# Batch 0's first DFT in whole float32, its result kept in chip memory and read from there

## The chip, the cores and the metric

The kernel runs on one NeuronCore of one Trainium2 chip. The metric is device time of one execution in microseconds: 2584.85 us, the median of three runs (2584.58 to 2585.59). Lower is better.

Names used below: PE (TensorE, the matmuls) and PEld (its weight loads), DVE (VectorE), ACT (ScalarE), POOL (GpSimd), SP (SyncE, which issues the DMAs). Chip memory means the on-chip memory of 128 partitions; DRAM is the memory outside the core.

## What is computed

A spectral layer on 8 batches of 3008 x 256, and behind it a feed-forward layer (FFN) on all 24064 rows:

```
X = rfft(x, axis=1)
Yr = Xr @ w_r - Xi @ w_i + b_r
Yi = Xr @ w_i + Xi @ w_r + b_i
Y  = shrink(Yr, 0.01) + 1j * shrink(Yi, 0.01)
y  = irfft(Y, n=3008, axis=1)
h  = y @ w_in          # 256 -> 2048
g  = h - tanh(h)
out = g @ w_out        # 2048 -> 256
```

The result is float32 and w_in and w_out are float64. Where the kernel needs the precision of float32 it either lets PE multiply whole float32 operands, or splits an operand into a high and a low part (type fp32r) and adds three matmuls: high x low, high x high, low x high.

## The kernel before

**The spectral layer by stages.** 3008 = 64 x 47, so the DFT of a batch is done in two steps. F1 (class `Forward`) is the DFT of length 47: x is laid out as [94 rows (two interleaved series of 47), 32 pairs, 256], and the table f1 [94, 96] turns 94 rows into 96. One step `q` treats two pairs, one matmul of N = 512. The result `a` has 32 pairs x 96 rows x 256. F2 (class `Spectrum`, for batch 0 its subclass `WholeSpectrum`) is the DFT of length 64: it needs the same row j of all 32 pairs on the partitions of chip memory, so F1's result is written to DRAM as `a` and read back in another order as `at`. The 96 rows of `a` are 4 groups of 24; a unit `jp` (12 units a batch) takes rows 2 jp and 2 jp + 1 of each group: 4 x 32 = 128 partitions and 2 x 256 columns. `rows` (L316) is this view of `a`. Behind F2 a unit does the products with w_r and w_i (`cross`), `shrink`, and the first step of the inverse DFT (`inverse`), and writes `z` to DRAM (`put`). Class `Unit` reads z back and makes the time rows that the FFN takes.

**Batch 0 at the start** (L930 to L972 and L973 to L1057). No FFN work exists yet, so batch 0 runs alone. PE first gets 11 matmuls on zeros (`idle(11)`), which keep it busy until x arrives. The 8 pieces of x are loaded at once. Each of the 16 steps (`steps`) splits its two pairs (ACT makes the high part, DVE the low), does three matmuls and one `idle(1)`, and `keep` copies the result from the accumulators into a buffer `st` and sends it to `a` in DRAM: 16 buffers taken in turn from three tags (th with 2, k with 5, tmp with 4). Between these writes the loads of the bias, w_i, w_r and i1 are issued. Then come `idle(16)` and the loop over 12 units: in iteration i unit i does F2 (`dft`), unit i - 1 `cross`, unit i - 2 `shrink`, unit i - 3 `inverse`; the load of `at` for unit i + 2 is issued in iteration i, into one of three buffers (tag `at`; the first held w_i). Weight pieces are loaded in iterations 0 (two), 4, 5, 8 and 9 (`raw_at`), halves of the table i2 in 5 and 8, and x of batch 1 in 9 and 10. `some` interleaves the conversion of weight pieces from float64.

**Order.** PE, ACT, DVE, POOL and SP run exactly the order in which the program issues their instructions (`manual_schedule`); semaphores come from the data. All DMAs of the program are issued by SP, in order: one that waits holds back all behind it.

**The weights.** `win_h`, `win_l` [128, 2, 2048] and `wout_h`, `wout_l` [128, 16, 256] hold w_in and w_out in two parts, 64 KB of each partition in all. They are filled in 16 pieces (`load_f64`, `split_f64`); pieces of part 0 and 1 are those of the FFN's first 8 of 16 blocks of 128. Pieces 0 to 5 are loaded in the unit loop, the others later, in `early`. `Chunk.up`, `Chunk.down`, `Pair.left` and `weight_sums` read them. The main part of the time is the loop over `Pair`s (L1163 on), where the FFN of one chunk and the spectral units of later batches alternate on PE.

**Buffers of DRAM.** `a` has two buffers that batches take in turn, `z` likewise.

Of the kernel before, what the change touches and what calls it, by code (L numbers as in the profile page):

```python
# [10 lines left out]
F32 = mybir.dt.float32  # L11
# [23 lines left out]
def dft_constants():  # L35
    _, m0 = index_maps()
    j = np.arange(NJ)
    n2 = np.arange(47)
    a = 2 * np.pi * np.outer(n2, j) / 47
    one = np.concatenate([np.cos(a), -np.sin(a)], 1)  # L40
    f1 = np.zeros((94, 96))
    f1[:47, :48] = one
    f1[47:, 48:] = one
    f1s = np.zeros((128, 96))
    f1s[:47, :48] = f1s[:47, 48:] = f1s[64:111, :48] = one
    n1 = np.array([2 * pair + par for par in range(2) for pair in range(NP)])
    th = 2 * np.pi * np.outer(n1, np.arange(128) % 64) / 64
    c, s = np.cos(th).reshape(2, NP, 128), np.sin(th).reshape(2, NP, 128)
    dr = np.stack([c, s], 2).transpose(1, 0, 2, 3).reshape(128, 128)
    di = np.stack([-s, c], 2).transpose(1, 0, 2, 3).reshape(128, 128)  # L50
    f2 = np.concatenate([dr[:, :96], dr[:, 32:], di[:, :96], -di[:, 32:]], 1)
    ph = 2 * np.pi * np.outer(np.arange(64), n1) / 64
    sg = np.where(np.arange(64) < 32, 1.0, -1.0)[:, None]
    c, s = np.cos(ph), np.sin(ph)
    i1 = np.zeros((2, 64, 2, 2, NP))
    i1[0, :, :, 0], i1[0, :, :, 1] = c.reshape(64, 2, NP), s.reshape(64, 2, NP)
    i1[1, :, :, 0], i1[1, :, :, 1] = (-sg * s).reshape(64, 2, NP), (sg * c).reshape(64, 2, NP)
    i1 = i1.transpose(0, 1, 4, 2, 3).reshape(128, 128)
# [12 lines left out]
    i2 = i2.transpose(1, 0, 2).reshape(128, -1)  # L71
    return [np.ascontiguousarray(v, np.float32) for v in (f1, f1s, f2, i1, i2)]


@with_exitstack
def spectral_ffn(ctx, tc, x, w_r, w_i, b_r, b_i, w_in, w_out, x_twice, f1, f1s, f2, i1, i2, out):
    nc = tc.nc
# [62 lines left out]

    win_h = const.tile([P, 2, FF], F32R, name="win_h")
    win_l = const.tile([P, 2, FF], F32R, name="win_l")
    wout_h = const.tile([P, NF, D], F32R, name="wout_h")
    wout_l = const.tile([P, NF, D], F32R, name="wout_l")

# [26 lines left out]
    def split_f64(part, k, raw):  # L172
        if k < 2:
            sl = slice(part * WB, (part + 1) * WB)
            hi_out, lo_out = win_h[:, k, sl], win_l[:, k, sl]
        else:
            n = WB // D
            f = part * WB // P + (k - 2) * n
            hi_out, lo_out = (w[:, f:f + n].rearrange("p t e -> p (t e)") for w in (wout_h, wout_l))
        top, low = raw[:, :, 1], raw[:, :, 0]  # L180
# [28 lines left out]
    class Forward:  # L209
# [4 lines left out]
        def load(self):  # L214
            if self.ch == 0:
# [15 lines left out]
        def dft(self, q):  # L231
            xh, xl = self.x[q]
            self.ps[q] = bank("ps_f1")
            pv = self.ps[q][:96].rearrange("p (a d) -> p a d", d=D)
            nc.tensor.matmul(pv, f1l, xh, start=True, stop=False)
            nc.tensor.matmul(pv, f1h, xh, start=False, stop=False)
            nc.tensor.matmul(pv, f1h, xl, start=False, stop=True)

        def keep(self, q, copy=nc.scalar.copy):
            if self.b == 0 or self.b == 1 and self.ch >= LOOK:  # L240
                n = 2
                pool, tag, bufs = ((ffn, "th", 2), (work, "k", 5), (work, "tmp", 4))[(2 * self.ch + q) % 3] if self.b == 0 else (load, "at", 3)
                st = pool.tile([96, 2, D], F32, name="st", tag=tag, bufs=bufs)
            else:
# [67 lines left out]
    class Spectrum:  # L312
# [6 lines left out]
        def load(self):  # L319
            if self.jp == 0:  # L320
                z_dram[self.b] = dram.tile([NP, 96, D], F32, name=f"z_{self.b}", tag="z")
            self.at = load.tile([P, 2, D], F32, name="at", tag="at", bufs=3)
            nc.sync.dma_start(out=self.at.rearrange("p j d -> p (j d)"), in_=rows(a_dram[self.b][0], self.jp))
            if self.b > 2:
# [7 lines left out]
        def transform(self):  # L332
            ps = self.ps = bank("ps_f2")
            pv = ps.rearrange("p (t r j m) -> p t j r m", t=2, r=2, j=2)
            for jj in range(2):
                o = m0[2 * self.jp + jj]
                rhs = f2t.rearrange("p (r u c) -> p r u c", r=2, u=2)[:, :, :, o:o + 32]
                for t in range(2):
# [183 lines left out]
    class Chunk:  # L522
# [27 lines left out]
        def up(self, f, i):  # L550
            n = self.n
            hp = H[0][:, i % 2, :n] if H else early_h[i % 2 if i < SINGLE else 0][:, :n]
            k = 0
            for lhs, rhs in ((win_l, self.yh), (win_h, self.yh), (win_h, self.yl)):
                for t in range(2):
                    nc.tensor.matmul(hp, lhs[:, t, f * P:(f + 1) * P], rhs[:, t, :n], start=k == 0, stop=k == 5)  # L556
                    k += 1
# [10 lines left out]
        def down(self, f, gh, gl, t):  # L568
# [8 lines left out]
            if f == 0 and self.c > 1:  # L577
                self.o[t] = ps_oo.tile([P, 512], F32, name=f"o{t}", tag=f"o{t}")
            for k, (lhs, rhs) in enumerate(((wout_l, gh), (wout_h, gh), (wout_h, gl))):
                nc.tensor.matmul(  # L580
                    self.o[t][:, :n], lhs[:, f, t * P:(t + 1) * P], rhs,
                    start=f == 0 and k == 0, stop=f == NF - 1 and k == 2,
                )
# [41 lines left out]
    class Pair:  # L625
# [13 lines left out]
        def left(self, name):  # L639
# [4 lines left out]
            t, f = {"a11": (0, 0), "a12": (1, 0), "a21": (0, 1), "a22": (1, 1)}[name]  # L644
            return [w[:, t, (2 * q + f) * P:(2 * q + f + 1) * P] for w in (win_h, win_l)]

# [51 lines left out]
    def weight_sums(p):  # L698
        wv = [w.rearrange("p k (q i m) -> p k i q m", i=2, m=P)[:, :, :, 2 * p:2 * p + 2] for w in (win_h, win_l)]
        pair = [work.tile([P, 2, 2, P], F32, name=f"ws{k}", tag="tmp", bufs=4) for k in range(2)]  # L700
# [233 lines left out]
    with tc.manual_schedule(engines={E.PE, E.Activation, E.DVE, E.Pool, E.SP}):  # L934
# [9 lines left out]

        idle(11)
        below = const.tile([P, 1], F32, name="below")
        nc.vector.memset(below, -LAM)
        f1h, f1l = split(load_whole(f1, [94, 96], "f1", tag="tmp", bufs=4), "f1", rest=nc.vector)
        first = [Forward(0, ch) for ch in range(NP // XC)]
        for f in first:  # L950
            f.load()
        f2t = load_const(f2, [P, 384], "f2")
        steps = [(f, q) for f in first for q in range(XC // 2)]
        loads = linear_loads()
        lin_in = next(loads)
        bias = lin_in[2]
        for i in range(len(steps) + 2):
            if 10 <= i < 14:
                next(loads)
# [279 lines left out]
```

## Time and profile before

| | |
|---|---|
| time before, median of three | 2584.85 us |
| profiled execution, its own time | 2586.71 us |
| its span (first to last instruction) | 2584.9 us |
| mean granted clock of PE over the span | 0.997 |
| busy: PE / DVE / ACT / POOL | 2557.7 / 1838.1 / 1608.0 / 792.4 us |
| moved by DMA | 235.87 MB, mean 91 GB/s |

The profile is of one execution. The chain is the work that ended last, followed back from the last instruction. A row of the chain in order of time has start, duration, engine, tile and line; a row of the timeline has start, duration, engine, line, operation, tiles, shapes and count, and in brackets how long the engine was idle before and what released it. A line of stretches has the stretch, its length, each engine's busy time with its count, the granted clock, the mean busy share of the 16 DMA engines, and GB/s. A row of a group has count, busy time, mean ns of one, and idle time before. A row of DMA issues has tiles, queue, count, KB each and the median time from issue to landing. A whole float32 matmul shows as two records.

### The profile page before, as it was taken

The page shows a single profiled execution, that of the slowest core. Times are in us where ns is not written, and L with a number is a line of the kernel's source. Part 1 is how long each engine was busy: PE and PEld are TensorE (multiplying, and loading weights), DVE is VectorE, ACT ScalarE, POOL GpSimd, SP SyncE. Part 2 cuts the span into 40 slices and gives each one's busy share as a digit, 9 for nine tenths or more (in the row PEclk, how much of TensorE's full clock was granted, in tenths as well). Part 3 has the DMA queues.
Part 4 walks back from the last instruction along what each step waited for, and adds up shares of the span by engine and source line. Part 5 has one row for each costly group of instructions (what it writes and reads, how often), then busy time and mean ns, then how long its engine had stood idle before and what let it go on. Part 6 is the DMA issues. An engine that isn't in the chain of part 4 may idle for free.

```text
span 2584.9 us, 42892 instructions
## 1 busy us (share of the span) xinstructions
PE 2557.7 (99%) x16041; PEld 2283.9 (88%) x16041; DVE 1838.1 (71%) x2742; ACT 1608.0 (62%) x2942; POOL 792.4 (31%) x885
## 2 busy tenths in 40 slices
PE   8999999999999999999999999999999999999999
PEld 6787898899889999899999999899998999999998
DVE  6787884777777776777776777767777666666665
ACT  5556566666666666666666666666666555565655
POOL 0004334332334433333324333333333323221210
PEclk8999999999999999999999999999999999999999
DMA  6521225233333332333323342232433121111000
GB/s 192 169 84 56 89 72 152 82 99 97 95 105 118 104 116 82 98 112 107 120 72 115 97 132 90 86 116 84 131 91 95 62 73 60 47 43 47 19 27 17
DMA packets 145521, 235.87 MB, mean 91 GB/s; under 512 B 12192, under 2 KB 85152, under 8 KB 145312
## 3 DMA queue, kind: packets, MB, share of 16 engines
q1 hardware_dynamic: 145312, 233.11, 28.8%
q8 instruction: 127, 2.08, 0.3%
q14 instruction: 82, 0.67, 0.1%
HBM read 142.36 MB, written 90.70 MB: 90 GB/s over the span
## 4 chain that ended last, share of the span: by engine, by line
PE 95%; DVE 2%; DMA 1%; ACT 1%; issue 0%; POOL 0%; SPq 0%; DVEq 0%; ACTq 0%; POOLq 0%
PE o L580 39%; PE H L651 34%; PE ps_v L366 5%; PE ps_i L507 4%; PE ps_f L339 3%; PE ps_t L366 2%; PE he L556 2%; PE ps_f L285 1%; PE ps_v L448 1%; PE ps_i L413 1%; PE ps_i L415 1%; PE ps_i L414 1%; DMA a<-st 1%; PE oe L580 1%; PE ps_t L448 0%; PE ps_i L471 0%
## 5 line engine op out<-in xcount | busy, mean ns | idle before, releaser
L689 ACT CAST gh<-th 128x1024 fp32r<-128x1024 f32 x352 | 371.4, 1055 | 381.8 <-DVE th L685 253.5
L651 PEld LDWEIGHTS H<-y_t,sum 128*128 128x128 f32 x3168 | 516.2, 188 | 102.3 <-DVE th L685 5.5
L580 PE MATMUL o<-gh,wout_l 128*128 128x512 f32 x1408 | 563.2, 400 | 0.0
L580 PE MATMUL o<-gl,wout_h 128*128 128x512 f32 x1408 | 554.3, 394 | 0.5 <-DVE gl L693 0.5
L580 PE MATMUL o<-gh,wout_h 128*128 128x512 f32 x1408 | 552.7, 393 | 0.0
L651 PE MATMUL H<-y_t,sum 128*128 128x256 f32 x3168 | 545.2, 281 | 0.9 <-DVE ot L593 0.7
L693 DVE TENSOR_TENSOR gl<-th,gh 128x1024 fp32r<-128x1024 f32 x352 | 440.6, 1252 | 57.6 <-ACT gh L689 54.8
L685 DVE TENSOR_TENSOR th<-H,th 128x1024 f32<-128x1024 f32 x352 | 428.3, 1217 | 5.0 <-ACT th L682 2.3
L682 ACT ACTIVATE th<-H 128x1024 f32<-128x1024 f32 x352 | 362.6, 1030 | 42.5 <-PE H L651 42.0
L667 DVE TENSOR_TENSOR H<-H,late 128x256 f32<-128x256 f32 x352 | 152.2, 432 | 319.5 <-PE H L651 283.3
L580 PEld LDWEIGHTS o<-gl,wout_h 128*128 128x128 f32 x1408 | 264.7, 188 | 60.8 <-DVE gl L693 1.5
L673 DVE TENSOR_TENSOR H<-H,late 128x256 f32<-128x256 f32 x352 | 151.7, 431 | 191.4 <-PE H L651 183.1
L651 PE MATMUL H<-y_b,win_h 128*128 128x256 f32 x1408 | 280.8, 281 | 0.0
L580 PEld LDWEIGHTS o<-gh,wout_l 128*128 128x128 f32 x1408 | 265.0, 188 | 7.9 <-ACT gh L689 0.5
L580 PEld LDWEIGHTS o<-gh,wout_h 128*128 128x128 f32 x1408 | 264.9, 188 | 7.3
L659 ACT COPY late<-H 128x256 f32<-128x256 f32 x352 | 131.6, 374 | 211.9 <-PE H L651 209.1
L651 PE MATMUL H<-y_more,win_h 128*128 128x256 f32 x1408 | 263.1, 279 | 0.0
L97 POOL TENSOR_TENSOR z_l<-mn,z_h 128x512 fp32r<-128x512 f32 x84 | 112.5, 1340 | 431.3 <-ACT z_h L96 276.4
L651 PEld LDWEIGHTS H<-y_more,win_h 128*128 128x128 f32 x1408 | 215.3, 188 | 6.1
L651 PEld LDWEIGHTS H<-y_b,win_h 128*128 128x128 f32 x1408 | 214.4, 188 | 0.2 <-POOL y_b L97 0.2
L651 PE MATMUL H<-y_more,win_l 128*128 128x256 f32 x704 | 201.1, 286 | 1.2 <-DVE H L673 1.2
L403 DVE TENSOR_TENSOR y<-tb,ps_v 64x256 f32<-64x256 f32 x384 | 160.8, 419 | 56.8 <-PE ps_v L366 44.8
(190 smaller groups left out, 4381.3 us busy)
## 6 DMA issues: line engine op xcount, KB each, us to landing
a<-st SPq DMA_DIRECT2D x188, 192.0 KB, 3.0
x<-in_x_twice SPq DMA_DIRECT2D x55, 512.0 KB, 4.7
at<-a SPq DMA_DIRECT2D x96, 256.0 KB, 3.2
z<-zo SPq DMA_DIRECT2D x96, 256.0 KB, 2.0
zin<-z SPq DMA_DIRECT2D x64, 384.0 KB, 4.4
out<-ot SPq DMA_DIRECT2D x47, 512.0 KB, 3.1
shared<-a SPq DMA_DIRECT2D x60, 256.0 KB, 3.7
shared<-in_i SPq DMA_DIRECT2D x58, 235.0 KB, 4.0
```

The lines of the kernel that those rows point to most:

```text
L97: rest.tensor_tensor(out=lo, in0=src, in1=hi.bitcast(F32), op=ALU.subtract)
L366: nc.tensor.matmul(dst, lhs[:, t], rhs[:, t, :], start=n == 0, stop=n == 5)
L403: nc.vector.tensor_tensor(out=y[ri * 64:(ri + 1) * 64, jj, :], in0=common(jj, ri), in1=self.vv[jj * 64:(jj + 1) * 64, ri * D:(ri + 1) * D] ...
L580: nc.tensor.matmul(self.o[t][:, :n], lhs[:, f, t * P:(t + 1) * P], rhs, start=f == 0 and k == 0, stop=f == NF - 1 and k == 2,)
L651: nc.tensor.matmul(dst, a, b, start=start and k == 0, stop=k == 2, skip_group_check=True)
L659: nc.scalar.copy(out=self.p7, in_=self.c11)
L667: nc.vector.tensor_tensor(out=self.c21, in0=self.acc, in1=self.p7, op=ALU.add)
L673: nc.vector.tensor_tensor(out=self.c22, in0=self.acc, in1=self.p7, op=ALU.add)
L682: nc.scalar.activation(out=self.th, in_=self.hp[:, :, :n], func=AF.Tanh)
L685: nc.vector.tensor_tensor(out=self.th, in0=self.hp[:, :, :self.n], in1=self.th, op=ALU.subtract)
L689: nc.scalar.copy(out=self.gh, in_=self.th)
L693: nc.vector.tensor_tensor(out=self.gl, in0=self.th, in1=h(self.gh), op=ALU.subtract)
```

## The change

- Batch 0's F1 is done with one whole float32 matmul a step on x as it was loaded (`f1f`, `self.xt`); the splits of x and the `idle(1)` go, and `idle(11)` at the start becomes `idle(6)`. The split table f1h, f1l is still made, for later batches.
- `keep` copies the result of batch 0 into `first_a` [96, 32, 256] in chip memory, in turn on ACT and DVE, and writes nothing to DRAM.
- `Spectrum.load` of batch 0 reads `first_a` by DMAs within chip memory. Unit 0 takes 8 DMAs, one for each group and row, from one partition each, half of them issued by ACT. The other units take two DMAs each, one for each row jj, from four partitions 24 apart (`first_a[row::NJ]`). The partitions of `at` are then in the order group, pair, so F2 of batch 0 has a table of its own with its rows in that order (`f2b`, input `f2_first`); f2t is loaded after the first two units' loads.
- The loads of f2b, bias, w_i, w_r and i1 are issued right behind those of x.
- The four weight tiles become two, `weights[0]` and `weights[1]`, each with half of the blocks of all four: [128, 4, 2048]. `first_a` has the memory of `weights[1]` (tag weights1), which is taken for the weights after batch 0's first time rows. `w_up` and `w_down` give the slices.

```diff
+    f2b = f2.reshape(NP, 4, 384).transpose(1, 0, 2).reshape(128, 384)
...
-    win_h = const.tile([P, 2, FF], F32R, name="win_h")
-    win_l = const.tile([P, 2, FF], F32R, name="win_l")
-    wout_h = const.tile([P, NF, D], F32R, name="wout_h")
-    wout_l = const.tile([P, NF, D], F32R, name="wout_l")
+    HF = NF // 2
+    weights = [const.tile([P, 4, HF * D], F32R, name="weights0")]
+    first_a = work.tile([96, NP, D], F32, name="a_first", tag="weights1", bufs=1)
+
+    def w_up(t, f, n=1):
+        lo = t * HF * P + f % HF * P
+        return [weights[f // HF][:, v, lo:lo + n * P] for v in range(2)]
+
+    def w_down(f, lo, n):
+        lo += f % HF * D
+        return [weights[f // HF][:, 2 + v, lo:lo + n] for v in range(2)]
...
         def dft(self, q):
-            xh, xl = self.x[q]
             self.ps[q] = bank("ps_f1")
             pv = self.ps[q][:96].rearrange("p (a d) -> p a d", d=D)
+            if self.b == 0:
+                nc.tensor.matmul(pv, f1f, self.xt[:94, 2 * q:2 * q + 2], start=True, stop=True)
+                return
+            xh, xl = self.x[q]
...
         def keep(self, q, copy=nc.scalar.copy):
-            if self.b == 0 or self.b == 1 and self.ch >= LOOK:
+            if self.b == 0:
+                p = self.ch * XC + 2 * q
+                copy(out=first_a[:, p:p + 2], in_=self.ps[q][:96].rearrange("p (a d) -> p a d", d=D))
+                return
+            if self.b == 1 and self.ch >= LOOK:
...
             self.at = load.tile([P, 2, D], F32, name="at", tag="at", bufs=3)
+            if self.b == 0:
+                for jj in range(2):
+                    row = 2 * self.jp + jj
+                    if self.jp < 1:
+                        for g in range(4):
+                            (nc.sync, nc.scalar)[g % 2].dma_start(out=self.at[32 * g:32 * g + 32, jj], in_=first_a[NJ * g + row:NJ * g + row + 1])
+                    else:
+                        nc.sync.dma_start(out=self.at[:, jj], in_=first_a[row::NJ])
+                return
...
-                rhs = f2t.rearrange("p (r u c) -> p r u c", r=2, u=2)[:, :, :, o:o + 32]
+                rhs = (f2b if self.b == 0 else f2t).rearrange("p (r u c) -> p r u c", r=2, u=2)[:, :, :, o:o + 32]
...
-        idle(11)
+        idle(6)
...
-        f2t = load_const(f2, [P, 384], "f2")
-        steps = [(f, q) for f in first for q in range(XC // 2)]
+        f2b = load_whole(f2_first, [P, 384], "f2", tag="spill", bufs=1)
         loads = linear_loads()
         lin_in = next(loads)
         bias = lin_in[2]
-        for i in range(len(steps) + 2):
-            if 10 <= i < 14:
-                next(loads)
-            if i == 14:
-                i1f = load_whole(i1, [P, P], "i1", tag="s_l")
+        for _ in range(4):
+            next(loads)
+        i1f = load_whole(i1, [P, P], "i1", tag="s_l")
+        f1h, f1l = split(f1f, "f1", rest=nc.vector)
+        steps = [(f, q) for f in first for q in range(XC // 2)]
+        for i in range(len(steps) + 1):
             if i < len(steps):
-                steps[i][0].split(steps[i][1], piece(2 + i % 4, [94, 2, 2, D], F32R, "x_first"), nc.vector)
-            if 1 <= i <= len(steps):
-                steps[i - 1][0].dft(steps[i - 1][1])
-                idle(1)
-            if i >= 2:
-                f, q = steps[i - 2]
-                f.keep(q, nc.vector.tensor_copy if i % 3 == 0 else nc.scalar.copy)
+                steps[i][0].dft(steps[i][1])
+            if i >= 1:
+                f, q = steps[i - 1]
+                f.keep(q, nc.vector.tensor_copy if i % 2 == 0 else nc.scalar.copy)
...
         for u in units[:2]:
             u.load()
+        f2t = load_const(f2, [P, 384], "f2")
...
+        weights.append(work.tile([P, 4, HF * D], F32R, name="weights1", tag="weights1", bufs=1))
         raw = work.tile([P, 2, 512], F32, name="raw", tag="raw", bufs=1)
```

The slices of the weights in `split_f64`, `up`, `down`, `left` and `weight_sums` are taken from `w_up`, `w_down` and `weights` in the same way.

More of the change, by code (lines that the diff above doesn't have):

```diff
@@ L71, in dft_constants, with spectral_ffn @@
     i2 = i2.transpose(1, 0, 2).reshape(128, -1)
-    return [np.ascontiguousarray(v, np.float32) for v in (f1, f1s, f2, i1, i2)]
+    return [np.ascontiguousarray(v, np.float32) for v in (f1, f1s, f2, f2b, i1, i2)]
 @with_exitstack
-def spectral_ffn(ctx, tc, x, w_r, w_i, b_r, b_i, w_in, w_out, x_twice, f1, f1s, f2, i1, i2, out):
+def spectral_ffn(ctx, tc, x, w_r, w_i, b_r, b_i, w_in, w_out, x_twice, f1, f1s, f2, f2_first, i1, i2, out):
     nc = tc.nc
@@ L173, in split_f64 @@
         if k < 2:
-            sl = slice(part * WB, (part + 1) * WB)
-            hi_out, lo_out = win_h[:, k, sl], win_l[:, k, sl]
+            hi_out, lo_out = w_up(k, part * WB // P, WB // P)
         else:
@@ L178, in split_f64 @@
             f = part * WB // P + (k - 2) * n
-            hi_out, lo_out = (w[:, f:f + n].rearrange("p t e -> p (t e)") for w in (wout_h, wout_l))
+            hi_out, lo_out = w_down(f, 0, WB)
         top, low = raw[:, :, 1], raw[:, :, 0]
@@ L214, in load @@
         def load(self):
-            if self.ch == 0:
+            if self.ch == 0 and self.b > 0:
                 a_dram[self.b] = dram.tile([2, NP, 96, D], F32, name=f"a_{self.b}", tag="a")
@@ L239, in keep @@
         def keep(self, q, copy=nc.scalar.copy):
-            if self.b == 0 or self.b == 1 and self.ch >= LOOK:
+            if self.b == 0:
[3 more added lines that the diff above has]
+            if self.b == 1 and self.ch >= LOOK:
                 n = 2
-                pool, tag, bufs = ((ffn, "th", 2), (work, "k", 5), (work, "tmp", 4))[(2 * self.ch + q) % 3] if self.b == 0 else (load, "at", 3)
-                st = pool.tile([96, 2, D], F32, name="st", tag=tag, bufs=bufs)
+                st = load.tile([96, 2, D], F32, name="st", tag="at", bufs=3)
             else:
@@ L553, in up @@
             k = 0
-            for lhs, rhs in ((win_l, self.yh), (win_h, self.yh), (win_h, self.yl)):
+            for v, rhs in ((1, self.yh), (0, self.yh), (0, self.yl)):
                 for t in range(2):
-                    nc.tensor.matmul(hp, lhs[:, t, f * P:(f + 1) * P], rhs[:, t, :n], start=k == 0, stop=k == 5)
+                    nc.tensor.matmul(hp, w_up(t, f)[v], rhs[:, t, :n], start=k == 0, stop=k == 5)
                     k += 1
@@ L578, in down @@
                 self.o[t] = ps_oo.tile([P, 512], F32, name=f"o{t}", tag=f"o{t}")
-            for k, (lhs, rhs) in enumerate(((wout_l, gh), (wout_h, gh), (wout_h, gl))):
+            wh, wl = w_down(f, t * P, P)
+            for k, (lhs, rhs) in enumerate(((wl, gh), (wh, gh), (wh, gl))):
                 nc.tensor.matmul(
-                    self.o[t][:, :n], lhs[:, f, t * P:(t + 1) * P], rhs,
+                    self.o[t][:, :n], lhs, rhs,
                     start=f == 0 and k == 0, stop=f == NF - 1 and k == 2,
@@ L644, in left @@
             t, f = {"a11": (0, 0), "a12": (1, 0), "a21": (0, 1), "a22": (1, 1)}[name]
-            return [w[:, t, (2 * q + f) * P:(2 * q + f + 1) * P] for w in (win_h, win_l)]
+            return w_up(t, 2 * q + f)
         def product(self, dst, left, right, start=False):
@@ L698, in weight_sums @@
     def weight_sums(p):
-        wv = [w.rearrange("p k (q i m) -> p k i q m", i=2, m=P)[:, :, :, 2 * p:2 * p + 2] for w in (win_h, win_l)]
+        wv = [weights[p // 2][:, v].rearrange("p (k q i m) -> p k i q m", k=2, i=2, m=P)[:, :, :, 2 * (p % 2):2 * (p % 2) + 2] for v in range(2)]
         pair = [work.tile([P, 2, 2, P], F32, name=f"ws{k}", tag="tmp", bufs=4) for k in range(2)]
@@ L943, in idle @@
                 nc.tensor.matmul(ps, warm[:, :P], warm, start=True, stop=True)
-        idle(11)
+        idle(6)
         below = const.tile([P, 1], F32, name="below")
         nc.vector.memset(below, -LAM)
-        f1h, f1l = split(load_whole(f1, [94, 96], "f1", tag="tmp", bufs=4), "f1", rest=nc.vector)
+        f1f = load_whole(f1, [94, 96], "f1", tag="tmp", bufs=4)
         first = [Forward(0, ch) for ch in range(NP // XC)]
@@ L1223 @@
     given["x_twice"] = given["x_twice"].reshape(B - 3, 128, NP, 2 * D)
-    given |= dict(zip(("f1", "f1s", "f2", "i1", "i2"), dft_constants()))
+    given |= dict(zip(("f1", "f1s", "f2", "f2_first", "i1", "i2"), dft_constants()))
     arrays, args = {}, []
```

## The prediction

> **What bounds the kernel now.** I read the page's head and its chain by engine, then the chain in order of time (start, duration, engine, tile, line).
>
> ```profile
> span 2584.9 us, 42892 instructions
> PE 95%; DVE 2%; DMA 1%; ACT 1%; issue 0%; POOL 0%; SPq 0%; DVEq 0%; ACTq 0%; POOLq 0%
> ```
>
> TensorE ends the chain for 95% of the span. So a microsecond is won only where the chain is not on PE, or where PE works below its clock. Both happen at the start:
>
> ```profile
> 7.49 8.67 DMA a<-st
> 20.55 5.22 DMA a<-st
> 26.49 3.92 DMA a<-st
> 30.55 2.72 DMA at<-a
> 33.40 3.76 PE ps_f L339 x16
> 37.88 3.71 PE ps_v L448 x8
> 41.59 1.42 PE ps_t L448 x4
> 43.01 0.89 PE ps_f L339 x8
> 43.90 0.42 PE ps_v L442
> 44.32 1.92 PE ps_v L448 x8
> 46.25 0.86 PE ps_t L448 x4
> ...
> 51.22 0.86 PE ps_i L471 x2
> ...
> 86.80 0.89 PE ps_f L339 x8
> ```
>
> Up to 33.40 us the chain lies mostly on DMAs: the first DFT's result out to `a` (three pieces), and back as `at`. From 43.01 it is PE alone. One unit of the following loop is 0.89 + 0.42 + 1.92 + 0.86 + 0.86 = 4.95 us of matmuls, and the last unit's F2 starts at 86.80, 43.79 us after the third unit's. The first two units cost more: their F2 takes 3.76 us for 16 instructions, where 8 take 0.89 later. Busy time in stretches (length, then PE, PEld, DVE, ACT, POOL, then clock, DMA share, GB/s) says why:
>
> ```profile
> 1.91:5.04 3.13, 3.13 (x7) 2.48 (x8) 0.25 (x1) 0.56 (x3) 0.00 (x0) 1.00 0.97 268
> 5.04:9.00 3.96, 3.96 (x18) 2.91 (x17) 2.97 (x5) 3.25 (x7) 0.00 (x0) 1.00 1.03 273
> 14.60:18.50 3.90, 1.13 (x5) 0.59 (x5) 1.14 (x2) 2.27 (x5) 0.00 (x0) 1.00 0.99 337
> 33.40:41.60 8.20, 8.20 (x26) 6.82 (x27) 2.97 (x7) 1.69 (x3) 0.00 (x0) 0.50 0.69 227
> ```
>
> The granted clock is 0.50 from 33.40 to 41.60, behind the wait for `at`. So the store and load of `a` cost PE twice: the wait, and half clock after it. In 14.60 to 18.50 PE worked 1.13 us of 3.90, because the copies to `st` waited for buffers that the queued writes had not freed.
>
> **The change, part by part.** All starts are of the profiled execution (2586.71 us around a span of 2584.9); I move the median, 2584.85, by the differences.
>
> *First DFT.* Removed: 16 ACT casts, 16 DVE subtractions, 48 matmuls in three passes, 16 warming matmuls between them, 16 DMAs of `a`. Added: 16 whole float32 matmuls of 94 rows by 512. The nearest row is L471 (128 rows by 512, float32, two records): 0.86 us each.
>
> ```profile
> 1.91 4.23 PE L943 MATMUL idle<-warm 128*128 128x512 f32 x11 [1.91 <-DVE below L947]
> 4.86 1.14 ACT L96 CAST x_first<-xt 94x512 fp32r<-94x512 f32 x2 [1.24 <-DMA xt<-in_x]
> 25.57 4.05 PE L943 MATMUL idle<-warm 128*128 128x512 f32 x17
> L249 ACT COPY st<-ps_f 96x512 f32<-96x512 f32 x11 | 6.4, 583 | 6.3 <-DMA a<-st 4.1 <-PE ps_f L237 2.2
> L249 DVE COPY st<-ps_f 96x512 f32<-96x512 f32 x5 | 3.4, 680 | 0.0
> ```
>
> The first x piece is there at 4.86, so the matmuls run from 4.86 to 4.86 + 16 x 0.86 = 18.6 if PE has its clock and x keeps up. In 5.04 to 9.00 the DMAs moved 273 GB/s, 1.44 us for a 384 KB piece, below the 1.72 us that PE needs for its two matmuls; this stage becomes PE's. The copies to `first_a` take 0.58 and 0.68 us on two engines in turn, hidden under 0.86 each; only the last shows: 18.6 + 0.14 + 0.68 = 19.5. The clock is the unknown: 7 matmuls ran in 1.91 to 5.04 (0.45 us each), 18 in 5.04 to 9.00 (0.22 each). Six warming matmuls in place of 11 work about 2.6 us and leave a short gap. Either the clock still rises near 5.04 (cost 0), or some 3.4 us later (the work done at half speed in that time is 1.7 us late); nothing here separates the ends, and I take the middle, 0.85.
>
> *F2's first loads.* Three steps of the old way (26.49 to 33.27) become one. Each queue, SP's and ACT's, issues four DMAs behind the last copy, at SP's pace of 0.41:
>
> ```profile
> 30.55 0.82 SPq L323 DMA_DIRECT2D at<-a  x2
> z<-zo SPq DMA_DIRECT2D x96, 256.0 KB, 2.0
> at<-a SPq DMA_DIRECT2D x96, 256.0 KB, 3.2
> ```
>
> A DMA from chip memory to chip memory is not in the trace. Its ends are `z<-zo` (2.0 from issue to landing) and `at<-a` (3.2); I take 2.0, since 32 KB is less than either. Half 0 lands at 19.5 + 0.8 + 2.0 = 22.3, half 1 at 23.1. The 16 warming matmuls (17 took 4.05) end at 18.6 + 3.8 = 22.4, so PE goes on without a long gap: F2 of unit 0 ends near 23.6. ACT's four issues hold back its cast of bias_top and `xf` by 1.6 us, inside the wait. What else stands behind the last copy is the work on w and the bias (first and last row of DVE, and POOL's):
>
> ```profile
> 27.68 0.69 DVE L128 SCALAR_TENSOR_TENSOR w_f<-wr_f,wi_f 128x512 f32<-128x512 f32 x1 [2.29 <-DMA wr_f<-in_w_r]
> 27.72 1.80 POOL L129 TENSOR_TENSOR w_f<-wi_f,wr_f 128x512 f32<-128x512 f32 x1 [26.89 <-DMA wr_f<-in_w_r]
> 31.20 0.29 DVE L97 TENSOR_TENSOR i_l<-i_f,i_h 128x128 fp32r<-128x128 f32 x1
> ```
>
> w is now queued right behind x and is there by then; the 3.8 us of DVE run from 19.5 to 23.3 and are used first near 26.4, so they cost nothing; had w come late, L442 would wait for them as F2 does for `at`.
>
> *The loads of units 1 to 11* are what I trust least. Each is two DMAs of 128 KB whose source is four partitions (rows 24 apart). How many DMA engines work on a DMA is seen at the first one, the table of 94 rows, before x begins; the other rows give the speed of an engine:
>
> ```profile
> 1.70:2.02 0.32, 0.11 (x1) 0.11 (x1) 0.16 (x2) 0.31 (x1) 0.00 (x0) 1.00 0.09 19
> 5.00:8.00 3.00, 3.00 (x14) 2.23 (x13) 1.98 (x3) 2.69 (x5) 0.00 (x0) 1.00 1.01 268
> 25.30:28.00 2.70, 2.70 (x13) 2.20 (x12) 0.41 (x2) 1.21 (x3) 0.28 (x1) 1.00 1.10 381
> 54.50:56.50 2.00, 2.00 (x10) 1.57 (x9) 1.93 (x5) 0.77 (x2) 0.00 (x0) 1.00 0.95 340
> ```
>
> The 94-row load kept 0.09 of 16 engines busy, 1.4 of them; loads of 96 and 128 rows keep all. The row count thus decides, and a source of four rows can hardly be cut over more than four engines. The ends are 4 and 16; I take 4. One engine moves 381/16/1.10 = 21.6 GB/s with rows of 1 KB, so 128 KB through four take 131072/4/21.6 = 1.52 us of each, 3.04 for a unit (0.38 and 0.76 if all 16 worked).
>
> [...]
>
> Now the queue of these four engines, from 22.2 (unit 1's first data) on, by sizes of the DMA table:
>
> ```profile
> w_raw<-in_moe_w_in SPq DMA_DIRECT2D x4, 512.0 KB, 6.3
> i<-in_i SPq DMA_DIRECT2D x2, 705.0 KB, 4.5
> ```
>
> At 340/16/0.95 = 22.4 GB/s the loads over all 16 engines cost each of them 1.46 (weights, 512 KB), 2.01 (i2), 0.73 (z), 0.55 (f2t, 192 KB). Unit 1 lands at 22.2 + 3.04 + 0.2 = 25.5, so PE waits two microseconds between units 0 and 1. Unit 2 lies behind f2t and two weight pieces: 22.2 + 3.04 + 0.55 + 2.92 + 3.04 + 0.6 = 32.3. PE would be ready at 25.5 + 0.89 + 3.20 = 29.6, or about 31.2 if the gap halves its clock for one stretch, so the load ends this wait and hides the clock's loss. F2 of unit 2 at 32.3 stands against 43.01: 10.7 us gained.
>
> From there PE needs 43.79 us to F2 of unit 11, at 76.1. Before that the four engines have 22 x 1.52 + 6 x 1.46 + 2 x 2.01 + 6 x 0.73 + 0.55 = 51.2 us of work, and 22.2 + 51.2 + 0.6 = 74.0. It fits with 2 us to spare: 96% full. SP's second issue of 0.41 in a unit of 4.95 is hidden.
>
> *The weights' new tiles* change addresses, not slices; loads from two different tiles cost the same 188 ns, so 0 from either side. weights1 waits for the last F2 load, long past when its first piece is split.
>
> ```profile
> L651 PEld LDWEIGHTS H<-y_t,sum 128*128 128x128 f32 x3168 | 516.2, 188 | 102.3 <-DVE th L685 5.5
> L651 PEld LDWEIGHTS H<-y_b,win_h 128*128 128x128 f32 x1408 | 214.4, 188 | 0.2 <-POOL y_b L97 0.2
> ```
>
> Sum: -10.7 + 0.85 = -9.85. Everything behind is ordered work on PE and moves along: 2584.85 - 9.85 = 2575.0.
>
> **The rivals.** *Sixteen engines after all* (or much faster ones): unit 1 lands with unit 0, no load is late, F2 of unit 2 comes at 28.3 to 30.5: gain 12.5 to 14.7, 2570 to 2572. Against it: the 0.09.
>
> *The four engines are the bound, mildly.* With 2 us to spare in 51, a unit's loads at 1.7 to 1.9 us each in place of 1.52 make F2 of unit 11 later by 22 x (t - 1.52) less the 2 us: gain 2 to 7, 2578 to 2583. For it: x came in at 268/16/1.01 = 16.6 GB/s per engine, 1.98 us for 128 KB by that row, so engines do run slower when several loads crowd; by that very rate the gain is about 2 us.
>
> [...]
>
> [...]
>
> *The change doesn't do what it says for the time*: F2 starts early but PE waits later for the same thing, the weights' pieces that now queue behind F2's loads; gain under 5 us either way. It is the mild rival's neighbour, priced with it.
>
> **How the numbers follow.** Forecast 0.53 (2572 to 2578); sixteen engines 0.12; mild bound 0.20, half of it at a gain over 5.2 us; near zero to a little slower 0.06; outright bound 0.09. 0.2% is 5.2 us, about what a measurement of this kernel can tell from no change. Faster: 0.53 + 0.12 + 0.07 = 0.72; slower 0.09 + 0.02 = 0.11; same 0.17. The range, 2571 to 2588, holds the forecast, the mild bound and the near-zero case, and leaves out the outright bound and the best of the sixteen.
>
> **What would show it.** Right: the matmuls of L235 become 16 of about 0.86 us back to back from 4.9 to about 19; no `a<-st` before 80 us; F2's first matmul near 22.5 at clock 1.00; F2 of unit 2 near 32 and released by a DMA; F2 of unit 11 near 76; loads of `at` at 128 KB taking over 3 us to land, with a DMA share near 0.25 where they run alone. Wrong: idle time before L339 in units 3 to 11 released by `at` (the four engines bound), clock 0.50 behind 23 us, or a first stretch of matmuls at 1.7 us each beyond 8 us.

## The result, and the profile after

| | before | after |
|---|---|---|
| time, median | 2584.90 us (2582.12 to 2585.89) | 2597.90 us (2589.74 to 2605.72) |
| ratio | 1 | 1.005, 95% interval 1.0028 to 1.0073 |
| profiled execution, its own time | 2586.71 us | 2605.45 us |
| its span | 2584.9 us | 2603.7 us |

The changed kernel is slower, and its eight executions fall in two groups: four from 2589.74 to 2592.82 and four from 2602.98 to 2605.72. The median, 2597.90, is the middle of the gap between them, (2592.82 + 2602.98) / 2, and no execution took about that long. The profiled one is of the upper group. The page of after, its span and its chain by engine:

```profile
span 2603.7 us, 42752 instructions
PE 96%; DVE 1%; DMA 1%; ACT 1%; issue 0%; POOL 0%; SPq 0%; DVEq 0%; ACTq 0%; POOLq 0%
```

The chain is on PE for 96%, as before for 95%: nothing new took PE's place as the bound. So most of the loss is in how fast PE worked. The chain of after in order of time (start, duration, engine, tile, line):

```profile
5.14 27.61 PE ps_f L242 x32
32.77 0.70 DVE a_first L252
33.54 2.82 DMA at<-a_first
...
37.08 5.24 DMA at<-a_first
42.36 1.23 PE ps_f L361 x4
43.59 0.72 PE ps_v L464
44.31 3.71 PE ps_v L470 x8
48.02 1.31 PE ps_t L470 x4
49.33 0.89 PE ps_f L361 x8
...
85.90 8.27 DMA at<-a_first
94.20 0.71 PE ps_f L361 x4
```

The first DFT's 16 matmuls (32 records) take 27.61 us, 1.73 each, where 0.86 was forecast. F2 of unit 2 starts at 49.33; before it was 43.01. So 6.3 us are lost by there, and 18.8 at the end of the span. Most of the rest, some 10 us, is lost where no instruction was changed. Stretches of 2000 us in the main loop (length, then busy time and count of PE, PEld, DVE, ACT, POOL, then clock, DMA share, GB/s), first before:

```profile
500.00:2500.00 2000.00, 1999.77 (x12990) 1813.07 (x12989) 1421.66 (x2056) 1264.81 (x2309) 663.56 (x745) 1.00 0.29 89
```

and after:

```profile
500.00:2500.00 2000.00, 1999.96 (x12930) 1810.53 (x12929) 1416.50 (x2051) 1259.19 (x2295) 658.89 (x737) 1.00 0.29 89
```

PE is busy throughout in both, at the same clock and the same DMA load, yet does 12930 matmuls in place of 12990: 60 fewer, 60 x 2000 / 12990 = 9.2 us. No wait shows this; the matmuls follow each other a little further apart. I call it the drift.

### The profile page after: what moved, and what is told of

It reads as the page before. It is cut to its first block, busy times and chain, and to the rows that moved or that the text cites. A ratio compares the mean times of both kernels' runs of the same rounds, so it can differ in the third digit from the quotient of the medians.

```text
span 2603.7 us, 42752 instructions
## 1 busy us (share of the span) xinstructions
PE 2580.6 (99%) x16004; PEld 2288.5 (88%) x16004; DVE 1828.9 (70%) x2729; ACT 1599.2 (61%) x2923; POOL 791.5 (30%) x885
## 4 chain that ended last, share of the span: by engine, by line
PE 96%; DVE 1%; DMA 1%; ACT 1%; issue 0%; POOL 0%; SPq 0%; DVEq 0%; ACTq 0%; POOLq 0%
PE o L603 39%; PE H L674 33%; PE ps_v L388 5%; PE ps_i L529 4%; PE ps_f L361 3%; PE ps_t L388 2%; PE he L578 2%; PE ps_f L298 1%; PE ps_f L242 1%; PE ps_v L470 1%; PE ps_i L436 1%; PE ps_i L437 1%; PE ps_i L435 1%; PE oe L603 1%; DMA at<-a_first 1%; PE ps_t L470 0%
## 5 line engine op out<-in xcount | busy, mean ns | idle before, releaser
L603 PE MATMUL o<-gh,weights 128*128 128x512 f32 x2816 | 892.3, 398 | 0.0
L603 PE MATMUL o<-gl,weights 128*128 128x512 f32 x1408 | 555.1, 394 | 0.5 <-DVE gl L716 0.5
L603 PEld LDWEIGHTS o<-gh,weights 128*128 128x128 f32 x2816 | 443.3, 188 | 16.2 <-ACT gh L712 0.5
L674 PE MATMUL H<-y_b,weights 128*128 128x256 f32 x2112 | 364.1, 281 | 0.0
L603 PEld LDWEIGHTS o<-gl,weights 128*128 128x128 f32 x1408 | 264.6, 188 | 63.2 <-DVE gl L716 1.4
L674 PE MATMUL H<-y_more,weights 128*128 128x256 f32 x2112 | 311.3, 283 | 1.2 <-DVE H L696 1.2
L674 PEld LDWEIGHTS H<-y_more,weights 128*128 128x128 f32 x2112 | 284.8, 189 | 16.3 <-DVE H L696 2.0
L674 PEld LDWEIGHTS H<-y_b,weights 128*128 128x128 f32 x2112 | 298.9, 188 | 0.0
L293 POOL TENSOR_TENSOR x<-x,x 64x512 fp32r<-64x512 f32 x55 | 71.2, 1294 | 257.1 <-issue 132.4
L683 ACT COPY H<-H 128x256 f32<-128x256 f32 x352 | 125.7, 357 | 11.2
```

The lines of the kernel that those rows point to most:

```text
L603: nc.tensor.matmul(self.o[t][:, :n], lhs, rhs, start=f == 0 and k == 0, stop=f == NF - 1 and k == 2,)
L674: nc.tensor.matmul(dst, a, b, start=start and k == 0, stop=k == 2, skip_group_check=True)
```

## The experiments

Two losses were to be explained, the clock in the first DFT and the drift. All medians below are with the kernel before run beside them (2585.4 to 2586.8), and the ratio is to that.

### The clock: more warming, and none

```diff
-        idle(6)
+        idle(11)      # e1_idle11
-        idle(6)       # e0_idle0
```

> The changed kernel with 11 warming matmuls at the start again in place of 6. Theory (the clock): in the profile after, 16 matmuls of F1 took 27.6 us (1.71 us each, twice the 0.86 forecast), because 6 warming matmuls did not raise the clock and the whole float32 matmuls could not; the two clusters of the times after (2590 to 2593 and 2603 to 2606) are the two cases. Then all runs are at 2589 to 2593, F1 takes 14 us, no run above 2600. Rival (a whole float32 matmul of N = 512 takes 1.71 us whatever the clock): F1 stays at 27.6 us and the times stay as after.

> The changed kernel with no warming matmuls at the start at all. Theory (the clock; whole float32 matmuls of 94 rows do not raise it by themselves): F1 takes 27.6 us in every run, 2602 to 2606, no run below 2600. Rival (some 3.4 to 7 us of any PE work raise it): F1 takes 16 to 18 us, 2591 to 2595.

e1_idle11: 2592.16 us (2590.59 to 2593.19), 1.0024 [1.0015, 1.0033]. e0_idle0: 2603.52 us (2602.55 to 2608.37), 1.0073 [1.0059, 1.0087]. PE's timeline of e0_idle0 (L242 is F1's matmul, L966 the warming matmul):

```profile
5.27 27.59 PE L242 MATMUL ps_f<-xt,f_f 94*96 94x512 f32 x32 [5.27 <-DMA xt<-in_x]
```

of after:

```profile
1.91 2.93 PE L966 MATMUL idle<-warm 128*128 128x512 f32 x6 [1.91 <-DVE below L970]
5.14 27.59 PE L242 MATMUL ps_f<-xt,f_f 94*96 94x512 f32 x32 [0.30 <-DMA xt<-in_x]
31.75 5.86 PE L966 MATMUL idle<-warm 128*128 128x512 f32 x16
```

and of e1_idle11:

```profile
1.91 4.10 PE L966 MATMUL idle<-warm 128*128 128x512 f32 x11 [1.91 <-DVE below L970]
6.19 13.95 PE L242 MATMUL ps_f<-xt,f_f 94*96 94x512 f32 x32 [0.17 <-DMA xt<-in_x]
19.57 4.21 PE L966 MATMUL idle<-warm 128*128 128x512 f32 x16
...
36.19 1.06 PE L361 MATMUL ps_f<-f_f,at 128*128 128x128 f32 x8
```

The same matmuls take 27.59 or 13.95 us. With no warming every run takes 2602.55 us or more, like the upper group of after; with 11 every run lies with the lower. So six warming matmuls raise the clock in some executions and not in others (by inference for the lower group, of which no execution was profiled), and the 16 whole float32 matmuls don't raise it themselves: they ran 27.6 us back to back at half speed. A stretch of after, in the columns above:

```profile
19.00:32.75 13.75, 13.75 (x18) 4.68 (x17) 2.75 (x4) 2.33 (x4) 0.47 (x1) 1.00 0.00 0
```

The column of the granted clock says 1.00 here and misleads: by the count, 18 records in 13.75 us where e1_idle11 has 32 in 13.95, PE is near half its rate. The 16 warming matmuls right behind F1 tell the same: they took 5.86 us in after, 4.21 in e1_idle11, so they began slow. In before the split matmuls of the same DFT ran at half clock for 3.4 us on end (18.66 to 22.03, granted clock 0.50 from 18.70 to 22.05) and at full clock behind that; 3.4 us is also the length that the prediction and the expectation of e0_idle0 take. Here 27.59 us were not enough: for this shape (94 rows, 96 columns, float32) work alone did not raise the clock. The type alone is not the reason: behind a later wait in e1_idle11 PE got nearly nothing but whole float32 matmuls of 128 rows, and F2 of 8 records went back to 1.06 us (36.19), where 4 had taken 1.23 at half clock (29.73). Nor is it clearly the shape: in before the split matmuls of 94 x 96, with one warming matmul in four among them, went from 0.63 us each (20.32 to 21.61) to 0.39 (from 22.30). Which property of the 16 it is was not tested.

e1_idle11 still pays half clock once, behind the wait for the first loads:

```profile
28.65:35.40 6.75, 5.67 (x14) 4.29 (x15) 2.46 (x6) 1.10 (x2) 0.00 (x0) 0.50 0.54 197
```

Even so its F2 of unit 2 stands 6.8 us ahead of before (36.19 against 43.01), and yet it ends 0.24% behind. Its count in 500 to 2500 us is 12929, as in after: the drift does not come from the start.

### The drift: layout alone, and its parts

The change moves the weights, and with them the working buffers behind. Four kernels took this apart. e2_layout is the kernel before with only its weights in the two new tiles; e3_order is e1_idle11 with the working buffers back at before's addresses; e5_far is e1_idle11 with the high and low parts 16 KB apart, as before; e7_plain0 is e1_idle11 with unit 0 loaded like the others.

```diff
-    win_h = const.tile([P, 2, FF], F32R, name="win_h")        # e2_layout (and the slices)
...
+    weights = [const.tile([P, 4, HF * D], F32R, name="weights0")]
+    weights.append(work.tile([P, 4, HF * D], F32R, name="weights1", tag="weights1", bufs=1))
...
-        f2b = load_whole(f2_first, [P, 384], "f2", tag="spill", bufs=1)        # e3_order
+        f2b = load_whole(f2_first, [P, 384], "f2", tag="sum2", bufs=1)
+        for k in range(3, 6):
+            nc.gpsimd.memset(piece(k, [P, 8], F32, "held"), 0.0)
...
-        return [weights[f // HF][:, v, lo:lo + n * P] for v in range(2)]       # e5_far
+        return [weights[f // HF][:, 2 * v, lo:lo + n * P] for v in range(2)]
...
-                    if self.jp < 1:                                            # e7_plain0
+                    if self.jp < 0:
```

> The kernel before with the weights alone moved: two tiles with half of the blocks of all four, the second one ahead of the working buffers, as in the change; first DFT, st and a as before. Between 500 us and the end the profile after falls back by 10 us against before, a little with every pair, while the instructions are the same. Theory A (where the weights lie): this kernel has that drift too, 2594 to 2596. Theory B (where the working buffers lie, which move in the change because the four buffers of x's parts are taken later and f2b takes the buffer spill early): no drift here, 2584 to 2586. Theory C (nothing of the kernel; the launch or the chip): no drift here either, but then e3 has one or not at random.

> e1 with the working buffers at the addresses of before: f2b takes the buffer sum2 and sum3 to sum5 are taken at once; the weights as in the change. Theory A (weights): like e1, 2589 to 2593. Theory B (working buffers): 10 us less than e1, 2579 to 2582, and faster than before. Theory C: like e1.

> e1 with the four parts of a weight tile in another order (w_in high, w_out high, w_in low, w_out low), so that high and low part of a slice are 16 KB apart as before, in place of 8 KB. Theory A2 (distance): 10 us less than e1, 2580 to 2583. Theory A1 (alignment) and A3: as e1, 2590 to 2593.

> e1 with unit 0's rows loaded as those of the other units: two DMAs from four partitions, in place of eight from one partition each on two queues. In e1's profile the eight took 0.7 us of SP each to issue and their packets 90 to 250 ns for 1 KB (46 elsewhere), and unit 0's second half landed 5.4 us behind the last copy. Theory (sixteen engines on one partition hold each other up, and the issues are dearer than the four-engine form): unit 0 lands 1 to 2 us sooner, units 1 and 2 too, time 1 to 3 us below e1. Rival (four engines are the slower form, as the code's own choice has it): 1 to 2 us above e1.

e2_layout: 2597.10 us (2593.05 to 2598.98), 1.0046 [1.0032, 1.006]; e3_order: 2592.80, 1.0029 [1.0017, 1.004]; e5_far: 2591.83, 1.0025 [1.0016, 1.0033]; e7_plain0: 2593.25, 1.0024 [1.0014, 1.0034]. The layout alone costs the kernel before 0.46%, some 11 us, and the stretch of e2_layout has about the count of after:

```profile
500.00:2500.00 2000.00, 2000.00 (x12926) 1810.23 (x12925) 1416.09 (x2048) 1260.11 (x2297) 661.04 (x743) 1.00 0.29 89
```

Neither putting the working buffers back, nor the distance of the two parts, nor loading unit 0 like the others changed the time of e1_idle11 by more than 1.1 us. What is left is where weights1 begins: behind `below`, a tile of 4 bytes that takes 32.

### The drift: the offset within 128 bytes

e6_shift moves nothing of the kernel before but `below`, to ahead of the weights, so that all of them begin 32 bytes later. e4_align is e1_idle11 with `rebias` taken ahead of weights1, which puts it 64 past a multiple of 128. e8_line is e3_order with `below` behind weights1; e9_lines moves `rebias` there too; e10_fill is e8_line with the start filled.

```diff
+    below = const.tile([P, 1], F32, name="below")             # e6_shift, ahead of win_h
-        below = const.tile([P, 1], F32, name="below")
...
+    rebias = work.tile([P, 1], F32, name="rebias", bufs=1)    # e4_align, ahead of first_a
...
     first_a = work.tile([96, NP, D], F32, name="a_first", tag="weights1", bufs=1)
+    below = work.tile([P, 1], F32, name="below", bufs=1)      # e8_line
+    rebias = work.tile([P, 1], F32, name="rebias", bufs=1)    # e9_lines
...
-        idle(16)                                              # e10_fill
+        idle(20)
...
-            load_raw(raw_at.get(i, 0))
+            if i > 0:
+                load_raw(raw_at.get(i, 0))
...
+            if i == 0:
+                load_raw(raw_at[0])
...
+            if i < 2:
+                idle((6, 4)[i])
```

> The kernel before with the 4-byte tile below ahead of the four weight tiles in place of behind them: all weights begin 32 bytes past a multiple of 64, nothing else moves. Theory A1 (alignment): all weights off where in e2 half of them are, so twice the drift, 2600 to 2606 (at the least as e2, 2595). A2 and A3: as before, 2584 to 2587.

> e1 with the 4-byte tile rebias taken ahead of first_a, so that weights1 begins at a multiple of 64 bytes (58304) in place of 32 past one (58272); weights0 is at such a multiple already, as all weights were before. The working buffers up to the old place of rebias move by 32 bytes too. Theory A1 (the drift comes from weights that begin 32 bytes off): no drift, 10 us less than e1, 2580 to 2583. Theory A2 (it comes from the distance of high and low parts, 8 KB in place of 16): as e1, 2590 to 2593. Theory A3 (another property of the place): as e1.

> As e3_order, but one 32-byte tile (below) is taken behind first_a and not ahead of the weights, so that the second half of the weights begins at a multiple of 128 bytes again, as all four weight tiles of the kernel before do; in e3_order it begins 32 bytes past one, in e4_align 64 past. If the drift of some 10 us over the FFN stage comes from weights that begin off a multiple of 128: no drift, so the lead of about 5 us at 500 us is kept, and the time is 2579 to 2583. If it comes from something else of the new layout: as e3_order, 2591 to 2596.

> As e8_line, but the second 32-byte tile (rebias) is taken behind first_a too, so that every working tile behind it moves by 32 bytes, to 64 past a multiple of 128, while the weights stay where e8_line has them. If only where the weights begin counts: as e8_line, 2579 to 2583. If the offset of the moving operands (y, g) counts as well: 5 us or more above e8_line.

> As e8_line, with the start filled: 20 warming matmuls in place of 16 ahead of F2, 6 and 4 behind F2 of units 0 and 1, and the first two weight pieces loaded behind unit 2's load, not ahead of it. If F2 of unit 2 in e1_idle11 was held by PE at half clock (28.65 to 35.48) and by the queue ahead of its load: no half clock there and F2 of unit 2 some 2 to 3 us earlier, 1.5 to 3 us below e8_line. If the time is given back later, in the unit loop: as e8_line within 1 us.

e6_shift: 2605.45 us (2604.18 to 2607.61), 1.0077 [1.0064, 1.0089]; 32 bytes cost 20 us with nothing else moved. e4_align: 2593.38, 1.003 [1.0019, 1.0042], no gain. e8_line: 2579.64 us (2578.06 to 2582.83), 0.9978 [0.9968, 0.9987]; e9_lines: 2579.60, 0.9977 [0.9967, 0.9986]. One tile of 32 bytes taken elsewhere wins 13 us on e3_order and turns the change into a gain (w1 to w3, the weights of the spectral products, move from 32 to 0 with it). The stretches, e6_shift:

```profile
500.00:2500.00 2000.00, 2000.00 (x12873) 1811.63 (x12872) 1410.27 (x2042) 1253.43 (x2288) 656.84 (x736) 1.00 0.29 89
```

and e8_line:

```profile
500.00:2500.00 2000.00, 1999.66 (x12998) 1811.91 (x12998) 1424.53 (x2056) 1263.44 (x2307) 664.51 (x745) 1.00 0.29 89
```

e10_fill: 2579.80 us (2577.68 to 2583.49), 0.9979 [0.997, 0.9987], as e8_line. Its start did what was meant, but by unit 11 little of that is left. PE's timeline of e8_line (F2 of unit 2, then the second half of unit 11's):

```profile
36.02 1.10 PE L362 MATMUL ps_f<-f_f,at 128*128 128x128 f32 x8
...
80.50 0.71 PE L362 MATMUL ps_f<-f_f,at 128*128 128x128 f32 x4 [0.50 <-DMA at<-a_first]
```

and of e10_fill:

```profile
33.85 1.06 PE L362 MATMUL ps_f<-f_f,at 128*128 128x128 f32 x8
...
80.74 0.71 PE L362 MATMUL ps_f<-f_f,at 128*128 128x128 f32 x4 [0.24 <-DMA at<-a_first]
```

2.2 us earlier at unit 2, 0.2 earlier at unit 11, where both wait for a load from `first_a`. So what PE wins before the loop it loses again inside it, nearly all of it; e10_fill's trace has PE waiting for these loads for 0.34 us at unit 3 (38.90) and 0.50 at unit 11.

### Is it 128 bytes, or one operand against the other?

e11_all (on e3_order) and e12_old (on the kernel before) put both small tiles at the very end, so that every other tile begins at a multiple of 128.

```diff
-        below = const.tile([P, 1], F32, name="below")
-        rebias = work.tile([P, 1], F32, name="rebias", bufs=1)
+        nc.gpsimd.memset(ffn.tile([P, 8], F32, name="held", tag="th"), 0.0)
+        small = ffn.tile([P, 2], F32, name="small", bufs=1)
+        below, rebias = small[:, 0:1], small[:, 1:2]
```

> As e8_line, but the two 32-byte tiles (below, rebias) become one at the very end of chip memory, so that every other tile, the sums of weights among them (sum0 to sum5, the weights of the 3168 matmuls of H from y_t), begins at a multiple of 128 bytes; in e8_line the working tiles begin 32 bytes past one. If an offset costs with every tile that PE takes as weights: those matmuls get 2 to 5 ns shorter from one to the next (118.9 ns in e8_line), 6 to 15 us in all, 2565 to 2574. If the working tiles' offset costs nothing, as e9_lines said of 64 against 32 bytes: as e8_line, 2578 to 2581.

> The kernel before with its two 32-byte tiles moved to the end in the same way and nothing else changed: every tile begins at a multiple of 128 bytes. If the offset costs with every weight tile: faster than before by what e11_all gains on e8_line and 2 to 4 us more (w1 to w3 and the sums together), 2567 to 2576, and e11_all stands 5 to 8 us below it, which is what the first DFT's change is worth by itself. If only the FFN's own weights count: as before, 2584 to 2587.

e11_all: 2596.36 us (2593.69 to 2597.11), 1.0036 [1.0022, 1.0049]; e12_old: 2598.61 us (2597.05 to 2600.90), 1.0047 [1.0035, 1.006]. Both expectations failed, and the theory of the multiple of 128 with them. I then sorted the matmuls of the runs so far by where their two operands begin within 128 bytes, the moving one and the one loaded as weights (LDWEIGHTS in the traces; places from the sizes and order of the tiles in the program). `H` is the FFN's first product, of y with the weights w_in or with sums of them made once (the sums); `o` is its second, of g with w_out; w1 to w3, made from w_r and w_i, multiply x, here the result of F2 of the later batches. Mean ns from one matmul's start to the next of the same kind with nothing between, in 500 to 2500 us:

| offsets of the two | o, 512 columns | H from the weights, 256 | w1 to w3 times x, 256 |
|---|---|---|---|
| alike | 233.3 (e11_all) | 118.9 (e11_all), 119.6 (e6_shift) | 120.0 (e11_all) |
| 32 or 96 apart | 234.2 (e6_shift) | 117.3 (before) | 118.8 (before) |
| 64 apart | 230.4 (before), 230.1 (e8_line) | 116.5 (e9_lines) | 114.1 (e8_line), 117.8 (e9_lines) |

So the new theory: matmuls are fastest where the two begin 64 apart, and for two of the three kinds slowest where they begin alike (`o` is slowest at 32). One execution shows it too: in e4_align `o` takes 230.3 ns with the weights' half 0 (64 apart from g) and 233.8 with half 1 (alike). And it says why e9_lines only equals e8_line: H from the weights got shorter there (117.6 to 116.5), H from the sums and w1 to w3 times x longer (116.9 to 117.9, 114.1 to 117.8). e13_apart and e14_old test it on tiles that never stood so (the sums of weights): sums first among the working tiles, behind them one tile of 64 bytes. Weights, sums and w1 to w3 are then at 0; y, x and g at 64.

```diff
+        for k in range(6):
+            nc.gpsimd.memset(piece(k, [P, 8], F32, "held"), 0.0)
+        small = work.tile([P, 16], F32, name="small", bufs=1)
+        below, rebias = small[:, 0:1], small[:, 1:2]
         zero = work.tile([P, 512], F32, name="zero", tag="k", bufs=5)
```

> As e8_line, with an order of the tiles in which the two operands of each of these matmuls begin 64 bytes apart within 128: weights, sums and w1 to w3 at 0, y, x and g at 64. e11_all had all of them at 0 and was slower, so the theory that weights must begin at a multiple of 128 has fallen. If what counts is the offset of the moving operand against the weights (by the matmuls from one to the next: o 230.1 to 230.4 ns at 64 apart, 233 to 234 at 0 or 32; H from the weights 116.5 at 64, 117.1 to 117.6 at 32, 118.8 to 119.6 at 0): H from the weights as in e9_lines, H from the sums, at 0 apart till now, 1 to 4 ns shorter, 4 to 15 us in all, 2565 to 2576. If it isn't: 2579 or more.

> The kernel before with the same offsets by the same edit (sums taken first among the working tiles, behind them one 64-byte tile with below and rebias). By the theory of the offsets: 2573 to 2581, and e13_apart stands 2 to 6 us below it, as e11_all stood 2.25 below e12_old; that difference is what the first DFT's change is worth where the addresses are alike. If the offsets of operands against each other don't count: 2584 or more.

e13_apart: **2573.30 us** (2570.89 to 2575.12), 0.9948 [0.9934, 0.9962]; e14_old: 2579.48 us (2577.57 to 2581.30), 0.9973 [0.9963, 0.9984]. Both times lie in the ranges expected, and H from the weights takes 116.6 ns, as in e9_lines (117.6 in e8_line). H from the sums missed its part: 116.3 ns in e13_apart and 116.9 in e8_line, where the two begin alike, 0.6 shorter and not 1 to 4. Being alike does not cost every kind the same. The stretch of e11_all, of e13_apart and of e14_old, in turn:

```profile
500.00:2500.00 2000.00, 1999.97 (x12911) 1813.86 (x12910) 1413.74 (x2046) 1258.49 (x2294) 661.93 (x743) 1.00 0.29 89
```

```profile
500.00:2500.00 2000.00, 1999.56 (x13034) 1810.74 (x13033) 1426.46 (x2061) 1268.80 (x2311) 666.14 (x745) 1.00 0.29 89
```

```profile
500.00:2500.00 2000.00, 1999.56 (x13032) 1811.00 (x13031) 1426.25 (x2060) 1268.86 (x2313) 668.45 (x748) 1.00 0.29 89
```

The count follows the offsets and not the start: e11_all and e12_old have 12911 and 12912, e13_apart and e14_old 13034 and 13032, though one of each pair has the changed first DFT and the other the old one. Laid beside each other, a kernel's offsets, in bytes past a multiple of 128:

| kernel | weights, half 0 / half 1 | y | sums | w1 to w3 | x | g | matmuls in 2000 us | time |
|---|---|---|---|---|---|---|---|---|
| e6_shift | 32 / 32 | 32 | 32 | 32 | 64 | 64 | 12873 | 2605.45 |
| e11_all, e12_old | 0 / 0 | 0 | 0 | 0 | 0 | 0 | 12911, 12912 | 2596.36, 2598.61 |
| e4_align | 0 / 64 | 64 | 64 | 32 | 64 | 64 | 12915 | 2593.38 |
| after, e1_idle11 | 0 / 32 | 32 | 32, 64 | 32 | 64 | 64 | 12930, 12929 | 2597.90, 2592.16 |
| e2_layout, e3_order | 0 / 32 | 32 | 32 | 32 | 64 | 64 | 12926, 12928 | 2597.10, 2592.80 |
| before | 0 / 0 | 32 | 32 | 32 | 64 | 64 | 12990 | 2584.90 |
| e8_line | 0 / 0 | 32 | 32 | 0 | 64 | 64 | 12998 | 2579.64 |
| e9_lines | 0 / 0 | 64 | 64 | 0 | 64 | 64 | 13002 | 2579.60 |
| e13_apart, e14_old | 0 / 0 | 64 | 0 | 0 | 64 | 64 | 13034, 13032 | 2573.30, 2579.48 |

What the change of the first DFT is worth with the clock raised and the same offsets is the difference of such a pair: 2579.48 - 2573.30 = 6.2 us here (2 to 6 were expected), 2.25 in e11_all against e12_old. Why the two disagree is open.

No run shows why the distance between the operands counts. The rule is rough, too: w1 to w3 times x stand 64 apart in e8_line and in e9_lines and take 114.1 and 117.8 ns, and `o` of the weights' half 0 takes 232.0 ns in after and 230.5 in e8_line with the same offsets. What else sets these is open.

## Why the prediction was wrong, point by point

The forecast was 9.85 us faster; the profiled span is 18.8 us longer, 28.6 off. In the order of its steps:

- **First DFT, the clock: failed.** "Either the clock still rises near 5.04 (cost 0), or some 3.4 us later" and "the middle, 0.85". In the upper group it rises at neither point: 16 x 1.73 in place of 16 x 0.86, about 13.8 us, 13 beyond the 0.85. The price of a matmul at full clock was right (13.95 us for 16 in e1_idle11, 0.87 each). The step carried over a clock that six warming matmuls did not reliably raise, and assumed that the float32 matmuls would raise it themselves.
- **F2's first loads: mis-sized.** From the end of the last copy (33.47) to F2 of unit 2 it took 15.9 us; 19.5 to 32.3 had been 12.8 in the forecast. The queues of after show an issue at 2.79 / 4 = 0.70 us on SP and 0.63 on ACT, where 0.41 was taken:

```profile
33.54 2.79 SPq L341 DMA_DIRECT2D at<-a_first  x4
33.54 2.52 ACTq L341 DMA_DIRECT2D at<-a_first  x4
...
42.36 1.23 PE L361 MATMUL ps_f<-f_f,at 128*128 128x128 f32 x4 [1.59 <-DMA at<-a_first]
```

  Unit 0 began at 37.47 and unit 1's second half at 42.36, and PE fell to half clock behind the wait. "The load ends this wait and hides the clock's loss" was wrong as well: e1_idle11's unit 2 was held by PE at half clock, not by its load. Together 3.1 us.
- **Loads of units 1 to 11: the engines and their rate right, the margin not.** Four engines, not 16. Where they run alone, after has a DMA share of 0.27, 0.27 x 16 = 4.3 engines, and 94 GB/s:

```profile
44.00:48.00 4.00, 4.00 (x10) 3.04 (x10) 2.46 (x6) 0.73 (x2) 0.00 (x0) 0.50 0.27 94
48.00:52.00 4.00, 4.00 (x21) 3.24 (x20) 2.16 (x6) 1.44 (x3) 0.00 (x0) 0.90 0.27 94
```

  94 / 4 = 23.5 GB/s of each engine makes 131072 / 4 / 23.5 = 1.39 us a DMA, for 1.52 forecast. That these are the same four engines for every load, as the queue's sum of 51.2 us takes it, no run shows; what after shows is a share that stays at 0.27, with 94 GB/s, over 10.8 us of these loads (44.00 to 54.80). The outright bound, given 0.09, did not appear: where the loads run alone they are faster than forecast. The "2 us to spare" were not there: from unit 1's last data to unit 11's it took 94.20 - 42.36 = 51.8 us in after, where 74.0 - 25.5 = 48.5 was forecast. e10_fill came 2.2 us early and lost nearly all of it; in after only about 1 us is lost in the loop (94.20 - 49.33 = 44.87 to unit 11's second half, where 43.79 was for its start).
- **The weights' new tiles, "0 from either side": failed.** This step decides the sign in the lower group: the layout alone costs 11 us (e2_layout). The row it argued from, 188 ns for a weight load from either tile, is unchanged after, and the duration of a matmul nearly so (`o`: 396 ns before, 397 after); what changed is the distance from one matmul to the next, which the step did not look at.
- **"Everything behind is ordered work on PE and moves along": failed for the same reason.** Of F2's gain in e1_idle11 (6.8 us) all was given back, and more: 5.1 us of it were left at the FFN's first matmul (109.9, before 115.0), and its span is 5.2 longer (2590.1 against 2584.9). What came behind that point was lost in instructions whose only edit is their addresses.

The sum of the misses: 13 + 3.1 + about 1 in the unit loop + 9 to 10 of drift, and a remainder of about 2 behind the unit loop, which is there by the FFN's first matmul (123.9, before 115.0) and was not followed up, against 28.6. None of the rivals named the clock or the addresses; the list of what would show it wrong did name both signs of the clock, the 1.7 us a matmul and the 0.50 behind 23 us. The shares differ by group: without the clock's 13 us the change stands at 2590 to 2593, still slower than before by the drift. Two of the prediction's smaller sums are off without moving the forecast: half of the mild bound's 0.20 is 0.10, where 0.07 went into the chance of faster, and the times of the sixteen engines, 2570 to 2572, leave out the 0.85 for the clock.

## What to carry to other kernels

A tile that moves others in chip memory is not free because the instructions stay the same (32 bytes cost 20 us in e6_shift): compare how many matmuls fit in a long stretch before and after, since neither the duration of one nor a wait shows the change, and try the small tiles elsewhere. Where work that kept PE's clock up is removed, ask of each matmul that remains whether it raises the clock (the 16 of float32 took 27.59 us in after and 13.95 in e1_idle11), and keep the warming until a trace shows that it is not needed. Here a gain ahead of a queue that was nearly full was given back in it: of 2.2 us in e10_fill 0.2 were left.

## What was not expected of the hardware

- Matmuls of 94 x 96 with 512 columns in float32 ran at half speed for 27.6 us on end (after, e0_idle0); 11 warming matmuls ahead of them halved that to 13.95 (e1_idle11).
- 32 bytes of offset under the weights changed this kernel by 20 us (e6_shift), through 2 to 4 ns from one matmul to the next (`o` 230.4 to 234.2, H from the weights 117.3 to 119.6). With the operands 64 bytes apart the kernel before alone gained 0.27% (e14_old), and with the change 0.52% (e13_apart, 2573.30 us, the fastest version).
